# Attention weights of three batches: turned by VectorE in 32x32 blocks and moved through device memory, in place of TensorE transposes

## The chip, the core and the metric

The kernel runs on one core of a Trainium2 chip. Its time is the device time of one execution in microseconds; before the change three runs took 450.7, 450.86 and 450.96 us, with a median of 450.86 us. One execution was also recorded by the hardware profiler. The engines are TensorE (PE, with PEld for its weight loads), VectorE (DVE), ScalarE (ACT), GpSimd (POOL) and SyncE (SP), which here issues every DMA.

## The reference

The reference is block-sparse attention followed by a gated two-layer network. The shapes are 4 batches, 8 heads, 768 tokens, head size 64, model size 512 and inner size 1024, in float32.

```python
k_sum = k.reshape(B, H, nb, block, D).max(axis=3)       # block = 32, nb = 24
v_sum = v.reshape(B, H, nb, block, D).mean(axis=3)
scores = concat([where(|i - j| < 16, q k^T / 8, -1e9), q k_sum^T / 8 + log(32)], -1)
a = exp(scores - max); a = a / (a.sum(-1) + 1e-9)
attn = a @ concat([v, v_sum], axis=2)                    # heads side by side -> x
xk = mu_k * x + (1 - mu_k) * x_prev;  xr = mu_r * x + (1 - mu_r) * x_prev
out = sigmoid(xr @ w_r) * (square(relu(xk @ w_k)) @ w_v)
```

A token's local keys lie within 15 positions, so 64 queries need 96 keys and 24 block summaries: 120 columns in all.

## The kernel before, in words

The attention is cut into 32 units, one for each batch, pair of heads and half of the sequence (384 tokens). The function `unit` (from line 443) makes one. It computes scores on PE (L458, 24 small matmuls) with the queries on the 128 partitions and the 120 keys along the row, three slots of 128 queries for each of the two heads. DVE adds the mask and finds the row's extreme (L469), ACT takes the exponential and its sum (L473), DVE inverts the sums (L479, L480) and POOL scales the rows (L485, six instructions). The weights lie in `y`, queries on the partitions. The product with the values needs keys on the partitions, so PE transposes the weights against an identity, two groups of three for a unit (L492, into the PSUM tile `pt`), and ACT copies each group to the tile `pts` (L496). PE then multiplies with the values (L505, 24 small matmuls), and DVE or ACT copies the result `av` into the tile `vx` that holds the tokens x (L516, L518).

The network works on halves of a batch: seven halves use the split form, in which each float32 operand is a sum of a high and a low part and three matmuls stand for one product. For a half there are a gate (L562 to L564, three groups of 12 matmuls), eight first products (L601, 12 matmuls each) and eight second products (L628, 9 each). ACT and DVE make the high and low parts of the activations (L542, L544, L614 to L616) and of the weights (L341, L344). The first half of batch 0 is partly plain: its gate (L575) and the products with an index below the two numbers `PLAIN` use the unsplit operands, 4 matmuls for a first product and 3 for a second. Plain float32 matmuls leave two records each in the profile, split ones one.

The kernel has no fixed order of its own. Every piece is declared to a planner (`Plan`, L106) with its engine, an estimated length, the tiles it reads and writes, and a due time; the planner plays the program through once and emits each engine's instructions in the order that it found. That order is then kept by the hardware: an engine whose next instruction must wait does nothing else. Constants at the top (L39 to L71) set the due times: `GATE0`, `GATE1` and `PERIOD` for the gates, `STEP0` and `STEP` for the products, `FIRST`, `SECOND` and `UNITS` for the units. The units of batch 1 to 3 are computed while the network works on the batch before. Matmuls on a tile of zeros (`warm`, L682) are put into gaps of PE that the planner foresees early on.

SP issues loads of k, v, q and vT (L359, L363, L441, L408), weights (L323) and stores of the output (L662). For batches 1 to 3 the block means of v are computed from the extra load vT and written into the windows of `vx` by two small DMAs for each set (L432, which spreads 24 rows over six windows).

## Time and profile before

| | |
|---|---|
| median of 3 runs | 450.86 us |
| profiled execution, its own time | 450.6 us |
| its span from first to last instruction | 448.8 us |
| PE busy | 441.7 us (98%) |
| ACT busy | 282.9 us (63%) |
| DVE busy | 261.2 us (58%) |
| POOL busy | 104.8 us (23%) |
| granted TensorE clock, mean | 1.000 |

The profiled time is 1.8 us longer than the span, for what lies around the first and the last instruction. PE's records overlap, because matmuls are pipelined, so the mean length of a matmul record (278 ns for a transpose) is longer than the distance from one start to the next. The distance between starts is what a matmul adds to a busy PE. In the rows of the timeline and of the chain of waits the first number is a start and the second a length, both in us.

### The profile page before, as it was taken

To read this page: it belongs to the slowest core of one execution; us is meant where nothing else is said; L and a number is where in the kernel's file an instruction comes from. 1 tells how busy PE (TensorE), PEld (TensorE's weight loads), DVE (VectorE), ACT (ScalarE), POOL (GpSimd) and SP (SyncE) were. 2 spreads that over 40 slices of the span, in tenths; PEclk is the share of its full clock that TensorE was granted. 3 is DMA by queue.
4 is the path that set the end of the run, shared out by engine and by line. 5 is a ranking of instruction groups with operands and counts; after the bars stand their busy time and mean duration, and the time that the engine had idled before them with its cause. 6 is when DMAs were issued, how large, how long until landed. Compare 5 with 4: busy or idle time off the path is not lost.

```text
span 448.8 us, 9629 instructions
## 1 busy us (share of the span) xinstructions
PE 441.7 (98%) x3521; PEld 366.3 (82%) x3521; DVE 261.2 (58%) x866; ACT 282.9 (63%) x808; POOL 104.8 (23%) x237
## 2 busy tenths in 40 slices
PE   8999999999999999999999999999999999999996
PEld 8755578778888888978888888987888888888895
DVE  3889998995645763194655756175663455232213
ACT  3798999997765583288866655268966555232221
POOL 0561545561540012032432012002442001000000
PEclk9999999999999999999999999999999999999999
DMA  8967886831024275051007076031000010001001
GB/s 288 395 225 253 318 300 225 273 136 39 15 71 150 77 246 200 2 169 31 15 2 272 2 243 229 0 125 64 15 15 15 1 71 1 1 0 72 0 0 72
DMA packets 24230, 51.96 MB, mean 116 GB/s; under 512 B 2935, under 2 KB 10743, under 8 KB 24183
## 3 DMA queue, kind: packets, MB, share of 16 engines
q1 hardware_dynamic: 24183, 51.35, 33.3%
q8 instruction: 28, 0.46, 0.4%
q14 instruction: 19, 0.16, 0.1%
HBM read 43.28 MB, written 6.29 MB: 110 GB/s over the span
## 4 chain that ended last, share of the span: by engine, by line
PE 90%; ACT 3%; DMA 3%; DVE 2%; SPq 1%; issue 0%; DVEq 0%
PE mm L628 30%; PE mm L601 29%; PE av L505 5%; PE pt L492 5%; PE sc L458 4%; PE mm L562 4%; PE mm L564 4%; PE mm L563 4%; DMA vx<-in_v 3%; PE mm L575 2%; ACT y L473 1%; PE pt L412 0%; DVE z L658 0%; ACT pts L496 0%; PE mm L397 0%
## 5 line engine op out<-in xcount | busy, mean ns | idle before, releaser
L601 PE MATMUL mm<-xs,w 128*128 128x384 f32 x756 | 147.4, 343 | 0.0
L601 PEld LDWEIGHTS mm<-xs,w 128*128 128x128 f32 x756 | 132.9, 188 | 7.4 <-issue 0.7
L485 POOL TENSOR_SCALAR y<-y,rc 128x120 f32<-128x120 f32 x192 | 83.9, 455 | 142.1 <-DVE rc L480 117.1
L628 PE MATMUL mm<-w,kh 128*128 128x512 f32 x366 | 100.3, 402 | 0.2 <-ACT kh L615 0.2
L608 ACT ACTIVATE r<-mm 128x384 f32<-128x384 f32 x64 | 31.3, 489 | 95.7 <-PE mm L601 95.7
L473 ACT ACTIVATE y<-y,mn 128x120 f32<-128x120 f32 x192 | 73.7, 387 | 13.2 <-DVE mn L469 13.1
L628 PEld LDWEIGHTS mm<-w,kh 128*128 128x128 f32 x366 | 66.1, 188 | 12.6 <-ACT kh L615 0.5
L614 DVE CAST kh<-r 128x384 fp32r<-128x384 f32 x55 | 21.1, 384 | 92.6 <-ACT r L610 83.6
L628 PE MATMUL mm<-w,kl 128*128 128x512 f32 x183 | 57.0, 406 | 0.0
L469 DVE CUSTOM_DVE_ANT_0 y<-sc,mask_sb 128x120 f32<-128x120 f32 x192 | 42.5, 276 | 16.1 <-PE sc L458 16.0
L544 DVE TENSOR_TENSOR xs<-xa,xs 128x384 fp32r<-128x384 f32 x56 | 30.5, 551 | 32.8 <-ACT xs L542 32.6
L628 PEld LDWEIGHTS mm<-w,kl 128*128 128x128 f32 x183 | 32.9, 188 | 7.4 <-issue 0.5
L533 DVE SCALAR_TENSOR_TENSOR xa<-vx,mu_sb,xa 128x384 f32<-128x384 f32 x56 | 33.5, 627 | 8.2 <-POOL xa L530 4.2
L616 DVE TENSOR_TENSOR kl<-r,kh 128x384 fp32r<-128x384 f32 x61 | 34.7, 569 | 4.2 <-ACT kh L615 0.7
L473 ACT ACTIVATION_READ_ACCUMULATOR y<-y,mn 128x1 f32 x192 | 36.4, 189 | 0.0
L610 ACT ACTIVATE r<-r 128x384 f32<-128x384 f32 x64 | 33.7, 526 | 1.2
L505 PEld LDWEIGHTS av<-pts,vx 120*64 120x64 f32 x768 | 25.1, 137 | 10.2 <-issue 6.4
L562 PE MATMUL mm<-w,xs 128*128 128x512 f32 x84 | 33.3, 397 | 0.0
L492 PE MATMUL pt<-ident_sb,y 128*120 128x128 f32 x192 | 32.5, 278 | 0.8 <-ACT pts L496 0.6
L496 ACT COPY pts<-pt 120x384 f32<-120x384 f32 x64 | 30.1, 470 | 5.0 <-PE pt L492 4.3
L564 PE MATMUL mm<-w,xs 128*128 128x512 f32 x84 | 32.9, 392 | 0.0
L563 PE MATMUL mm<-w,xs 128*128 128x512 f32 x84 | 32.8, 390 | 0.0
(65 smaller groups left out, 505.1 us busy)
## 6 DMA issues: line engine op xcount, KB each, us to landing
vx<-in_v SPq DMA_DIRECT2D x32, 384.0 KB
kt<-in_k SPq DMA_DIRECT2D x15, 544.0 KB
qt<-in_q SPq DMA_DIRECT2D x32, 192.0 KB
out<-z SPq DMA_DIRECT2D x24, 256.0 KB
st<-in_vT SPq DMA_DIRECT2D x12, 384.0 KB
st<-in_w_k SPq DMA_DIRECT2D x8, 512.0 KB
st<-in_w_v SPq DMA_DIRECT2D x8, 512.0 KB
st<-in_w_r SPq DMA_DIRECT2D x4, 512.0 KB
```

What stands on the lines that cost most here:

```text
L469: op("DVE", "mask", None, lambda h=h, i=i, var=var: nc.vector.tensor_tensor_reduce(out=y[h].t[:, i, :], in0=sc[h].t[:, i, 0:NK], in1=mask_ ...
L473: op("ACT", "exp", None, lambda h=h, i=i: nc.scalar.activation(y[h].t[:, i, :], y[h].t[:, i, :], AF.Exp, bias=mn[h].t[:, i:i + 1], scale=-1.0,
L485: op("POOL", "norm", None, lambda h=h, i=i: nc.gpsimd.tensor_scalar(out=y[h].t[:, i, :], in0=y[h].t[:, i, :], scalar1=rc.t[:, NSL * h + i: ...
L492: nc.tensor.transpose(out=pt[h].t[0:NK, i * P:(i + 1) * P], in_=y[h].t[:, i, :], identity=ident_sb)
L505: nc.tensor.matmul(av.t[hs, w * QW:(w + 1) * QW], windows(vw)[:, w, hs], pts[h].t[:, i, c * QW:(c + 1) * QW], start=True, stop=True,)
L562: nc.tensor.matmul(ps.t, xh.t[:, ts], h, start=(p == 0), stop=False)
L563: nc.tensor.matmul(ps.t, xh.t[:, ts], l, start=False, stop=False)
L564: nc.tensor.matmul(ps.t, xl.t[:, ts], h, start=False, stop=(p == NPAIR - 1))
L601: nc.tensor.matmul(ps.t[:, 0:HT], w.t[:, p * P:(p + 1) * P], x[p][s].t, start=(n == 0), stop=(n == len(terms) * NPAIR - 1))
L610: op("ACT", "square", None, lambda: nc.scalar.activation(r.t, r.t, AF.Square), reads=[(r, 0)], writes=[(r, 0)])
L616: op("DVE", "sub", None, lambda: nc.vector.tensor_tensor(out=kl.t, in0=r.t, in1=kh.t.bitcast(F32), op=ALU.subtract), reads=[(r, 0), (kh, 0 ...
L628: nc.tensor.matmul(acc[t].t, a.t[:, t * P:(t + 1) * P], v.bitcast(F32) if single else v, start=start, stop=stop)
```

## The change

For batches 1 to 3 the six PE transposes and the two ACT copies of a unit are gone. In their place stand:

- two DVE instructions (`flip`, new line 514), one for each head, each of which turns the 12 blocks of 32x32 in a 128x384 tile. The `y` tiles grow from 120 to 128 columns, so that they divide by 32, and POOL clears the eight added columns once. The turned blocks go into a tile of the pool `st`, which the loads of weights and of vT use too.
- four stores (`put`, new line 523), each from 32 partitions to a scratch tile in device memory (`far`, four tiles), 128 runs of 768 bytes each. The place in the scratch does what the block transpose leaves undone: it exchanges the blocks.
- one load (`get`, new line 527) of the 128 x 3072 bytes back into `pts`, which is now one tile for both heads, with two tiles in turn.

Batch 0 keeps the PE transposes. Its copies write the new arrangement of `pts`, and the products with the values read each 64 queries as two runs of 32.

The planner's numbers change too: `PLAIN` goes from 3 to 6, so that three more first and three more second products of the first half are plain; the steps, periods and gaps of the due times change; and the scores of batches 1 to 3 are due 22 us ahead of their unit's time, in place of 10.

```diff
-STEP0 = 4000
-PLAIN = 3, 3
-GATE1 = 76000
-PERIOD = 50000
-STEP = 4600
-SLACK = 400
+STEP0 = 5200
+PLAIN = 6, 6
+GATE1 = 84000
+PERIOD = 52000
+STEP = 4400
+SLACK = 800
...
-GAP = 300
+GAP = 500
...
+AHEAD = 22000
+ISSUES = dict(put=720, get=400, spread=820)
...
-UNITS = 5500
+UNITS = 8500
...
-        op("PE", "score", due - 10000, scores, reads=[*e["kparts"], (kt, "s"), (qt, 0)],
+        op("PE", "score", due - (10000 if b == 0 else AHEAD), scores, reads=[*e["kparts"], (kt, "s"), (qt, 0)],
...
+            if b > 0:
+                continue
             op("PE", "transpose", due - 3500 + 800 * h, transposes,
                reads=[(y[h], i) for i in range(NSL)] + [*IDENT], writes=[(pt[h], 0)])
             op("ACT", "pts", None, lambda h=h: nc.scalar.copy(
-                out=pts[h].t, in_=pt[h].t[0:NK, 0:NSL * P].rearrange("p (i c) -> p i c", c=P)),
-               reads=[(pt[h], 0)], writes=[(pts[h], 0)])
+                out=pts.t[0:NK, :, h].rearrange("p a i q -> p i a q"),
+                in_=pt[h].t[0:NK, 0:NSL * P].rearrange("p (i a q) -> p i a q", i=NSL, a=4)),
+               reads=[(pt[h], 0)], writes=[(pts, h)])
+        spots = [(pts, h) for h in range(2)]
+        if b > 0:
+            yt = buf("st", U32, False)
...
+            for h in range(2):
+                op("DVE", "flip", due - AHEAD + 8000 + 600 * h, lambda h=h: nc.vector.transpose(
+                    out=turned()[:, :, h], in_=y[h].t.rearrange("p i (r c) -> p r i c", r=4)),
+                   reads=[(y[h], i) for i in range(NSL)], writes=[(yt, h)])
+            far = buf("far")
...
+            for c in range(4):
+                op("SP", "put", due - 8000 - ISSUES["put"] * (3 - c), lambda c=c: nc.sync.dma_start(
+                    out=rows()[:, :, c], in_=turned()[32 * c:32 * c + 32].rearrange("p r h i q -> p r (h i q)")),
+                   reads=[(yt, 0), (yt, 1)], writes=[(far, c)], size=32 * 3072)
+            spots = [(pts, "all")]
+            op("SP", "get", due - 4500, lambda: nc.sync.dma_start(
+                out=pts.t.rearrange("p c h i q -> p (c h i q)"), in_=far.t.rearrange("p c n -> p (c n)")),
+               reads=[(far, c) for c in range(4)], writes=spots, size=P * 3072)
...
-                        av.t[hs, w * QW:(w + 1) * QW], windows(vw)[:, w, hs], pts[h].t[:, i, c * QW:(c + 1) * QW],
+                        av.t[hs, w * QW:(w + 1) * QW], windows(vw)[:, w, hs], pts.t[0:NK, 2 * c:2 * c + 2, h, i],
```

The order of the instructions moves with it. On PE, in the network's second half of batch 1 while a unit of batch 2 is computed, the order before has this stretch: one group of transposes, six matmuls of a second product, the other group, and the next unit's scores.

```order
L492 MATMUL pt_130<-ident_sb,y_93 120x128 x3
L628 MATMUL mm_133<-w_0_616,kh_119 128x512
L628 MATMUL mm_133<-w_0_688,kh_119 128x512
L628 MATMUL mm_135<-w_0_616,kh_119 128x512
L628 MATMUL mm_135<-w_0_688,kh_119 128x512
L628 MATMUL mm_132<-w_0_616,kh_119 128x512
L628 MATMUL mm_132<-w_0_688,kh_119 128x512
L492 MATMUL pt_130<-ident_sb,y_94 120x128 x3
L458 MATMUL sc_128<-kt_61,qt_65 64x120 x2
```

In the changed program the same kind of stretch holds the products with the values (new line 536) alone among the network's matmuls.

```order
L659 MATMUL mm_130<-w_0_720,kh_117 128x512
L659 MATMUL mm_130<-w_0_751,kh_117 128x512
L659 MATMUL mm_132<-w_0_720,kh_117 128x512
L659 MATMUL mm_132<-w_0_751,kh_117 128x512
L659 MATMUL mm_133<-w_0_720,kh_117 128x512
L659 MATMUL mm_133<-w_0_751,kh_117 128x512
L536 MATMUL av_129<-pts_105,vx_70 64x64 x12
L659 MATMUL mm_130<-w_0_720,kl_119 128x512
```

The 48 transpose groups of batches 1 to 3 are gone from PE; what the values wait for is now a load.

On SP the units' DMAs stand among the others. This is the piece in which the first two units of batch 2 are put out and loaded back (`far` and `pts` are the scratch and its destination; `vx<-vm` spreads the block means).

```order
L523 DMA far_136<-st_121 32x4x192 x4
L527 DMA pts_104<-far_136 128x768
L523 DMA far_137<-st_122 32x4x192
L436 DMA vx_76<-vm_87 24x6x128
L523 DMA far_137<-st_122 32x4x192 x3
L436 DMA vx_79<-vm_87 24x6x128
L412 DMA st_121<-in_vT 128x768
L445 DMA qt_66<-in_q 128x384
L527 DMA pts_105<-far_137 128x768
```

SP issues 286 DMAs in place of 166: 96 stores and 24 loads are added and none of the others is taken away. SP too keeps its order: a load back waits for its four stores, and whatever stands behind it on SP waits with it.

On DVE the turns stand between the network's work. This piece is from the same two units (`kl` is the low part of an activation that a second product needs, `sm` and `rc` the sums of the second unit).

```order
L514 STREAM_TRANSPOSE st_121<-y_93 128x4x96
L647 TENSOR_TENSOR kl_119<-r_115,kh_117 128x384
L514 STREAM_TRANSPOSE st_121<-y_91 128x4x96
L483 TENSOR_SCALAR sm_100<-sm_100 128x6
L484 RECIPROCAL rc_103<-sm_100 128x6
L645 CAST kh_116<-r_114 128x384
L647 TENSOR_TENSOR kl_118<-r_114,kh_116 128x384
L514 STREAM_TRANSPOSE st_122<-y_92 128x4x96
```

A turn waits for POOL's scaling of its tile, and the low parts behind it in the queue wait with it. Counted over the whole order, DVE gets 48 turns; copies of `av` on DVE go from 12 to 4 and on ACT from 20 to 28, casts of activations on DVE from 55 to 41 and on ACT from 6 to 17; ACT's copies to `pts` go from 64 to 16.

More of the change, by code (lines that the diff above doesn't have):

```diff
@@ L184, in schedule @@
                         continue
-                    start, need, ok = max(at, now, o.due - EARLY if e == "SP" else 0), {}, True
+                    start, need, ok = max(at, now, o.due - EARLY if e == "SP" and o.name not in ("put", "get") else 0), {}, True
                     if e == "SP":
@@ L228, in schedule @@
             if e == "SP":
[L229 removed]
+                engines[e] = start + ISSUES.get(o.name, ISSUE)
                 dma = max(dma, start + 600) + o.size * DMA_NS_PER_BYTE
@@ L446, in unit @@
         sm, rc = buf("sm"), buf("rc")
-        pt = [buf("pt") for _ in range(2)]
-        pts = [buf("pts") for _ in range(2)]
+        pts = buf("pts")
+        pt = [buf("pt") for _ in range(2)] if b == 0 else None
         av = buf("av")
```

29 lines of the change are left out of this document (18 added, 11 removed).

## The prediction

> **What bounds the kernel now.** I read the page's head and its chain of waits first, then busy time by stretches, then the waits of PE.
>
> ```profile
> span 448.8 us, 9629 instructions
> PE 441.7 (98%) x3521; PEld 366.3 (82%) x3521; DVE 261.2 (58%) x866; ACT 282.9 (63%) x808; POOL 104.8 (23%) x237
> PE 90%; ACT 3%; DMA 3%; DVE 2%; SPq 1%; issue 0%; DVEq 0%
> ```
> ```profile
> 0.00:40.00 40.00, 37.72 (x443) 27.02 (x444) 30.30 (x105) 27.85 (x88) 14.47 (x36) 1.00 0.81 291
> 40.00:100.00 60.00, 59.13 (x520) 42.77 (x519) 58.11 (x203) 57.43 (x178) 31.20 (x56) 1.00 0.74 257
> 100.00:350.00 250.00, 250.00 (x2083) 213.24 (x2083) 139.49 (x494) 164.50 (x479) 57.81 (x146) 1.00 0.27 90
> 350.00:446.00 96.00, 94.81 (x480) 83.26 (x478) 33.26 (x66) 33.09 (x66) 1.32 (x1) 1.00 0.06 20
> ```
> ```profile
> PE mm L628 <- ACT kh L615: 0.2, 1, 0.2
> ```
>
> The columns of the stretches are the stretch, then busy time of PE, PEld, DVE, ACT and POOL, the clock, the DMA share and GB/s. From 100 us on PE has no gap, and the last row, PE's only wait between 100 and 446 us, is 0.2 us. So there a microsecond of PE work taken away is a microsecond gained, as long as nothing makes PE wait instead. From 40 to 100 us PE, DVE (58.11 of 60) and ACT (57.43) are all full. Before 40 us loads rule (DMA share 0.81) and PE is padded with warm matmuls. The clock is 1.00 in all four.
>
> **What goes: 48 transpose groups on PE.** One transpose group is three matmuls; its price is a distance of starts, not the 278 ns of a record.
>
> ```profile
> 106.45 0.49 PE L492 MATMUL pt<-ident_sb,y 128*120 128x128 f32 x3
> 106.87 0.85 PE L458 MATMUL sc<-kt,qt 64*64 64x120 f32 x24
> 329.27 0.85 PE L458 MATMUL sc<-kt,qt 64*64 64x120 f32 x24
> 330.04 0.92 PE L505 MATMUL av<-pts,vx 120*64 120x64 f32 x24
> 330.89 0.96 PE L628 MATMUL mm<-w,kl 128*128 128x512 f32 x3
> 331.69 0.49 PE L492 MATMUL pt<-ident_sb,y 128*120 128x128 f32 x3
> 331.94 2.33 PE L601 MATMUL mm<-xs,w 128*128 128x384 f32 x12
> 334.11 0.49 PE L492 MATMUL pt<-ident_sb,y 128*120 128x128 f32 x3
> ```
>
> The group costs 0.25 us (331.69 to 331.94) to 0.42 us (106.45 to 106.87). It also makes its neighbours a little longer: the first product behind it takes 2.17 us (331.94 to 334.11) where 2.11 is usual. A second reading bounds the whole from above, by the period of a batch with units and the stretch without any:
>
> ```profile
> 253.97 0.39 PE L562 MATMUL mm<-w,xs 128*128 128x512 f32 x1
> 358.68 0.39 PE L562 MATMUL mm<-w,xs 128*128 128x512 f32 x1
> 444.64 0.40 PE L628 MATMUL mm<-w,kl 128*128 128x512 f32 x1
> ```
>
> One batch takes 104.7 us (253.97 to 358.68). The last batch, which has no units beside it, takes 86.4 us (358.68 to 445.0), of which about 2.1 us is a second product left from the batch before: 84.3 us. Eight units with their four means thus cost 20.4 us. Scores are 0.77 (329.27 to 330.04) and values 0.85 (330.04 to 330.89), 13.0 us for eight; with some 0.8 us for the means 6.6 us are left for 16 groups, 0.41 us each. I take 0.36, between the 0.32 that the middle of 0.25 and 0.42 gives and 0.41: 48 x 0.36 = **17.3 us** off (15.4 to 19.7).
>
> **What comes on PE: PLAIN from 3 to 6.**
>
> ```profile
> 41.73 2.58 PE mm L601 x8
> 47.86 2.58 PE mm L628 x6
> 169.12 2.10 PE mm L628 x9
> 171.21 2.11 PE mm L601 x12
> ```
>
> These pieces of the chain are a plain first and second product (2.58 us each) and split ones (2.11 and 2.10). Three of each: 3 x (0.47 + 0.48) = **2.85 us** on. Against it three fewer high and low parts are made on the crowded DVE; I count nothing for that, since the new order puts the turns of batch 1 and earlier scores into the same time.
>
> **What comes on DVE, and what leaves ACT.** The trace shows no block transpose. Its nearest rows are elementwise instructions of the same 128x384:
>
> ```profile
> L616 DVE TENSOR_TENSOR kl<-r,kh 128x384 fp32r<-128x384 f32 x61 | 34.7, 569 | 4.2 <-ACT kh L615 0.7
> L614 DVE CAST kh<-r 128x384 fp32r<-128x384 f32 x55 | 21.1, 384 | 92.6 <-ACT r L610 83.6
> L516 DVE COPY vx<-av 128x384 f32<-128x384 f32 x12 | 6.7, 555 | 8.1 <-PE av L505 8.1
> L496 ACT COPY pts<-pt 120x384 f32<-120x384 f32 x64 | 30.1, 470 | 5.0 <-PE pt L492 4.3
> ```
>
> Between 384 and 569 ns I take 0.56 us, the slow end, because blocks are no plain stream: 48 x 0.56 = 27 us on DVE. The planner moves 8 copies (8 x 0.555) and 14 casts (14 x 0.384) off DVE, 9.8 us. DVE then has about 278 us of work in some 437, and ACT, without 48 copies of 0.47 (22.6 us), has less than before. Neither bounds the whole; PE's 100 to 350 us cover this work, where DVE was busy 139 of 250. If the cover failed it would be by a turn that waits for POOL while the low parts queue behind it, and then PE waits for those. In the piece of the order shown the turns come after the next unit's masks, so POOL has had that time.
>
> [...]
>
> **The new way from scores to values.** Here a wait can take the place of the work. The old chain of one unit, and the nearest DMAs:
>
> ```profile
> 337.65 0.85 PE L458 MATMUL sc<-kt,qt 64*64 64x120 f32 x24
> 341.88 2.46 POOL L485 TENSOR_SCALAR y<-y,rc 128x120 f32<-128x120 f32 x6 [5.48 <-DVE rc L480]
> ```
> ```profile
> L432 SPq DMA_DIRECT2D vx<-vm x24: 778/786/949, 83.3 to 339.9; - x24
> 0.74 0.86 SPq L359 DMA_DIRECT2D kt<-in_k  x2
> 3.36 0.55 DVE L373 TENSOR_REDUCE kg<-kt 128x24 f32<-128x384 f32 x1 [3.36 <-DMA kt<-in_k]
> 4.20 0.55 DVE L373 TENSOR_REDUCE kg<-kt 128x24 f32<-128x384 f32 x1 [0.21 <-DMA kt<-in_k]
> 445.09 1.03 SPq L662 DMA_DIRECT2D out<-z  x2
> ```
>
> Scores start at 337.65 and POOL ends at 344.34: 6.7 us. The second turn adds 0.56 and perhaps 0.3 in DVE's queue: 7.6. Four stores follow. The nearest issue is the spread of the means, 786 ns for 24 x 6 runs (a put has 128 runs), so the last store is issued 2.4 us after the first. How long a DMA takes: a load of 280 KB, issued at 0.74, woke DVE at 3.36, 2.6 us; with the second part, 544 KB, it was 4.20, 3.5 us; the last stores of 256 KB, issued by 446.1, were over by the span's end at 448.8, at most 2.7 us. A store of 96 KB lies below the loads by its size, and with its longer issue I take 2.5 us (2.1 to 2.7). The load back of 384 KB lies between the two loads; I take 2.9 us (2.6 to 3.5). Sum: 7.6 + 2.4 + 2.5 + 2.9 = 15.4 us, about 15.7 with semaphores.
>
> SP can add to it: one or two spreads of 0.79 stand between a unit's stores and its load, so 16.5 to 17.3 us; and where a sigmoid came before, ACT loads its table for exponentials first (1.28 us):
>
> ```profile
> L473 ACT ACT_TABLE_LOAD x9 | 11.5, 1283 | 0.9 <-PEq L795 0.7
> ```
>
> Against that stands the PE work which the new order puts between the start of a unit's scores and its values. For the first unit of batch 2 it is three groups of scores (3 x 0.77), four first products (4 x 2.11), three and two thirds of second ones (3.67 x 2.10) and one means transpose (0.2): 18.7 us. Counted like this over all 24 units it is 17.5 to 23.7 us, 21 in the middle; the shortest is the fourth unit of batch 1. So the loads should land 1 to 4 us before they are needed, with little to spare in a few units. When PE waits once, the scores that are already out gain the same time, so a late load is not paid again by the units in flight. I put **1.5 us** for all such waits (0 to 8).
>
> **The start.** The order of the first 40 us is almost the same, with 44 warm matmuls for 39 and the same gate. The planner thus sees about five more small gaps there. Each warm matmul is two records:
>
> ```profile
> L682 PE MATMUL pt<-zero_sb 128*128 128x128 f32 x78 | 13.2, 323 | 1.6 <-POOL vx L514 1.0 <-ACT pts L496 0.6
> ```
>
> 13.2 us for 39 are 0.34 us each; five make 1.7 us at most, if none of it fills time that was idle anyway, and nothing if all of it does. I take **0.5 us**.
>
> **Sum.** The profiled execution took 450.6 us (span 448.8 and 1.8 around it). 450.6 - 17.3 + 2.85 + 1.5 + 0.5 = 438.15 us. The median of the three runs is 0.26 us above the profiled one, so I forecast **438.4 us**, 2.8% less.
>
> **Rivals.**
>
> *The load is late in many units.* If store and load take 1.5 us longer each than I put, the way is 19 to 20 us, and about half of the 24 units (those with under 21 us of PE work) are late by 1 us or a little less, some 8 to 10 us in place of 1.5: 446 us. For it: no row shows a load that follows a store to device memory, and SP's order puts other transfers ahead. Against: the DMA share is 0.27 from 100 to 350 us, so the queues are mostly empty.
>
> *SP becomes the bound, and the kernel is slower.* SP keeps its order, so the wait of each load back for its four stores holds the loads of q, k and v behind it; these feed the next scores, and the delay goes round. It decides from the point where the way exceeds the mean 21 us of PE work by over half a microsecond in every unit, that is when store and load together take about 11 us and not 5.4: 24 x 0.6 = 14 us eat the gain. At 1 us for each unit the sum is 438.4 - 1.5 + 24 = 461 us. Against it is the 2.7 us bound on a store above. [...]
>
> *The neighbours' time goes too, and nothing waits.* 48 x 0.41 off, no late loads, no loss at the start: 450.86 - 19.7 + 2.85 = 434.0 us.
>
> *The change does not do what it says* (the transposes stay on PE) is excluded by the new order: 48 PE transposes are left of 192, all of batch 0.
>
> **How the numbers follow.** The forecast (435.5 to 442 us) gets 0.58, late loads in many units 0.18, the better case 0.12, SP as the bound 0.12. A measurement of this kernel tells a change of about 0.2%, 0.9 us. Only the slower rival crosses that line, and its lower edge meets no change: faster 0.86, within it 0.04, slower 0.10. The range leaves out what lies above late loads and a little below the better case: 433.5 to 447.
>
> **What would show it.** PE's busy time should fall by about 14 us, the L601 and L628 rows should stay at their lengths, and PE's waits for the DMA of `pts` should sum to under 3 us. Turns should read 0.4 to 0.6 us and a put's issue about 0.75 us. The forecast is wrong if `values` wait for `pts` by more than a microsecond in most units, if DVE shows waits for POOL's `y` in front of `kl`, or if the first product starts more than 2 us later than 41.7 us.

## The result, and the profile after

The changed kernel takes 445.62 us (median of four runs, 444.78 to 447.34), against 450.84 us for the kernel before beside it: a ratio of 0.9889, 95% interval 0.9855 to 0.9923. It is faster by 5.2 us; the forecast was 12.4. The sign and the place of the gain were right, its size was more than twice too large. The profiled execution took 446.4 us, where the sum had been 438.15, so 8.25 us are to be found.

The head of the page and its chain of waits:

```profile
span 444.6 us, 9448 instructions
PE 433.3 (97%) x3366; PEld 351.4 (79%) x3366; DVE 274.5 (62%) x890; ACT 269.1 (61%) x772; POOL 109.4 (25%) x245
PE 80%; DMA 9%; ACT 6%; DVE 3%; issue 1%; SPq 0%; ACTq 0%
```

PE still sets the end, but its share of the chain fell from 90% to 80%, and DMA has 9% of it where it had 3%. None of these 9% are stores or loads back; the long pieces behind the start are loads of weights and of k and a spread (start, length):

```profile
54.10 5.84 DMA st<-in_w_k
64.06 4.88 DMA st<-in_w_k
82.08 5.13 DMA kt<-in_k
99.87 2.37 DMA vx<-vm
102.24 2.34 issue
```

From 47 to 99.8 us the chain has 18.8 us of ACT, the 15.9 us of these three loads, 8.0 us of PE and 7.8 of DVE; in the kernel before it has 37.3 us of PE there and no load. PE's busy time fell by 8.4 us (441.7 to 433.3), not by the 14 forecast. Busy time by stretches (stretch, then PE, PEld, DVE, ACT, POOL, the clock, the DMA share, GB/s):

```profile
40.00:100.00 60.00, 57.97 (x455) 35.89 (x455) 56.70 (x200) 54.80 (x173) 27.25 (x57) 1.00 0.78 252
100.00:350.00 250.00, 247.33 (x2010) 208.83 (x2010) 158.09 (x519) 156.15 (x451) 59.52 (x144) 0.99 0.54 165
100.00:110.00 10.00, 7.33 (x66) 5.64 (x66) 6.99 (x25) 7.53 (x25) 3.16 (x9) 0.83 0.70 193
```

From 100 to 350 us PE was busy for all 250 before; now 2.7 us are missing, all of them in the ten microseconds from 100 to 110, and there the granted clock is 0.83. The waits of PE say on what:

```profile
PE av L536 <- issue: 2.7, 1, 2.7
PE mm L606 <- DVE xs L564: 1.4, 1, 1.4
```

Of 24 products with the values that wait for a load back, one waited: the second unit of batch 1, for 2.7 us. Rows of PE's timeline around it (start, length; rows in between are left out):

```profile
104.57 1.02 PE L536 MATMUL av<-pts,vx 120*64 120x64 f32 x24 [2.67 <-issue]
105.53 1.22 PE L659 MATMUL mm<-w,kh 128*128 128x512 f32 x2
106.55 0.63 PE L659 MATMUL mm<-w,kl 128*128 128x512 f32 x1
106.97 0.63 PE L593 MATMUL mm<-w,xs 128*128 128x512 f32 x1
108.67 0.40 PE L594 MATMUL mm<-w,xs 128*128 128x512 f32 x1
110.52 0.62 PE L659 MATMUL mm<-w,kh 128*128 128x512 f32 x2
```

The matmuls behind the wait are slower than the same ones later (records of 0.63 against 0.40; 1.22 for two against 0.62). The seven from 105.53 to 108.67 take 3.14 us; at the later rate (0.23 from start to start) they take 1.60. So the wait cost 2.67 us and 1.5 more in a slow clock. Microsecond by microsecond the clock reads 0.62 from 105, 0.50 from 106 and from 107, 0.67 from 108 and 1.00 from 109.

The way of this unit from scores to values shows where it was late; its scores and its second turn are these rows:

```profile
80.80 0.85 PE L462 MATMUL sc<-kt,qt 64*64 64x120 f32 x24
91.66 0.57 DVE L514 STREAM_TRANSPOSE st<-y 128x384 f32<-128x384 f32 x1
```

From the start of the scores to the end of the second turn it takes 11.4 us (80.80 to 92.23), where the sum had 7.6. The whole way to the values takes 23.8 us (to 104.57), and without the wait there were 21.1 us of PE's time for it, the middle that the prediction had counted.

The new row of DVE among the groups of instructions, and from PE's timeline the two starts that bound a batch and PE's last matmul:

```profile
L514 DVE STREAM_TRANSPOSE st<-y 128x384 f32<-128x384 f32 x48 | 27.4, 572 | 11.0 <-POOL y L489 7.9 <-POOL vx L545 1.6 <-DMA qt<-in_q 1.2
```
```profile
254.28 0.39 PE L593 MATMUL mm<-w,xs 128*128 128x512 f32 x1
354.35 0.39 PE L593 MATMUL mm<-w,xs 128*128 128x512 f32 x1
440.49 0.40 PE L659 MATMUL mm<-w,kl 128*128 128x512 f32 x1
```

A turn takes 0.572 us and 48 take 27.4. A batch with units takes 100.07 us (254.28 to 354.35), where it took 104.71: 4.64 us for 16 groups, 0.29 each and not 0.36.

Last, the start, on PE and on DVE:

```profile
41.72 2.84 PE L606 MATMUL mm<-w,xs 128*128 128x512 f32 x6 [1.41 <-DVE xs L564]
44.40 2.74 PE L632 MATMUL mm<-xs,w 128*128 128x384 f32 x8
```
```profile
39.88 0.95 DVE L377 TENSOR_REDUCE kg<-kt 128x48 f32<-128x768 f32 x1 [1.04 <-DMA kt<-in_k]
41.80 2.20 DVE L564 SCALAR_TENSOR_TENSOR xs<-vx,mu_sb,xs 128x384 f32<-128x384 f32 x4
```

The first plain product starts at 44.40; before it was 41.56. DVE stood 1.04 us in front of a reduction over keys whose load had not landed, and the mixes (L564) that PE's gate needs were queued behind it. Not all of the 2.84 us is lost: ahead of this point PE now makes one unit's scores more (144 small matmuls in place of 120, 0.77 us), which it is spared later.

The two executions can be compared at three points: the first plain product, the first gate of batch 1 (the expectations below call it the first product of the second channel mix), and PE's end.

| kernel | first plain product | gate of batch 1 | from there to PE's end |
|---|---|---|---|
| before | 41.56 | 149.29 | 295.75 |
| after | 44.40 | 154.19 | 286.70 |

Behind the gate of batch 1 both kernels have the same matmuls, except for the 32 groups. There the change is a clean gain of 9.05 us, 0.28 for each group. Up to that gate it has lost 4.9 us, although 16 of the 48 groups lie there.

### The profile page after: what moved, and what is told of

The parts are those of the page before. It is cut to its first block, busy times and chain, and to the rows that moved or that the text cites. A ratio compares the mean times of both kernels' runs of the same rounds, so it can differ in the third digit from the quotient of the medians.

```text
span 444.6 us, 9448 instructions
## 1 busy us (share of the span) xinstructions
PE 433.3 (97%) x3366; PEld 351.4 (79%) x3366; DVE 274.5 (62%) x890; ACT 269.1 (61%) x772; POOL 109.4 (25%) x245
## 4 chain that ended last, share of the span: by engine, by line
PE 80%; DMA 9%; ACT 6%; DVE 3%; issue 1%; SPq 0%; ACTq 0%
PE mm L659 28%; PE mm L632 27%; PE av L536 5%; PE mm L593 4%; PE mm L595 4%; PE mm L594 4%; PE sc L462 4%; DMA st<-in_w_k 2%; ACT y L477 2%; DMA kt<-in_k 2%; PE mm L606 2%; DMA mu_sb<-in_mu 1%; DMA vx<-in_v 1%; DMA qt<-in_q 1%; ACT wc L328 1%
## 5 line engine op out<-in xcount | busy, mean ns | idle before, releaser
L632 PE MATMUL mm<-xs,w 128*128 128x384 f32 x744 | 149.1, 349 | 0.0
L632 PEld LDWEIGHTS mm<-xs,w 128*128 128x128 f32 x744 | 130.8, 188 | 10.5 <-issue 1.9
L489 POOL TENSOR_SCALAR y<-y,rc 128x120 f32<-128x120 f32 x192 | 85.4, 462 | 139.8 <-DVE rc L484 109.7
L659 PE MATMUL mm<-w,kh 128*128 128x512 f32 x348 | 94.6, 400 | 0.4 <-ACT kh L646 0.4
L659 PEld LDWEIGHTS mm<-w,kh 128*128 128x128 f32 x348 | 64.3, 189 | 13.1 <-ACT kh L646 0.7
L645 DVE CAST kh<-r 128x384 fp32r<-128x384 f32 x41 | 15.4, 375 | 69.8 <-ACT r L641 69.7
L659 PE MATMUL mm<-w,kl 128*128 128x512 f32 x174 | 54.4, 406 | 0.0
L561 POOL TENSOR_SCALAR xa<-vx,om_sb 128x384 f32<-128x384 f32 x16 | 12.4, 785 | 105.3 <-DVE xs L575 102.2
L647 DVE TENSOR_TENSOR kl<-r,kh 128x384 fp32r<-128x384 f32 x58 | 32.7, 564 | 7.2 <-ACT kh L646 4.4
L564 DVE SCALAR_TENSOR_TENSOR xa<-vx,mu_sb,xa 128x384 f32<-128x384 f32 x56 | 33.3, 619 | 2.7 <-ACT xa L558 2.7
L514 DVE STREAM_TRANSPOSE st<-y 128x384 f32<-128x384 f32 x48 | 27.4, 572 | 11.0 <-POOL y L489 7.9
```

What stands on the lines that cost most here:

```text
L489: op("POOL", "norm", None, lambda h=h, i=i: nc.gpsimd.tensor_scalar(out=y[h].t[:, i, 0:NK], in0=y[h].t[:, i, 0:NK], scalar1=rc.t[:, NSL * ...
L564: op("DVE", "mixd", None, lambda: nc.vector.scalar_tensor_tensor(out=xa.t, in0=xt.t[:, 1 + lo:1 + lo + HT], scalar=mu_sb[:, which, p:p + 1 ...
L632: nc.tensor.matmul(ps.t[:, 0:HT], w.t[:, p * P:(p + 1) * P], x[p][s].t, start=(n == 0), stop=(n == len(terms) * NPAIR - 1))
L647: op("DVE", "sub", None, lambda: nc.vector.tensor_tensor(out=kl.t, in0=r.t, in1=kh.t.bitcast(F32), op=ALU.subtract), reads=[(r, 0), (kh, 0 ...
L659: nc.tensor.matmul(acc[t].t, a.t[:, t * P:(t + 1) * P], v.bitcast(F32) if single else v, start=start, stop=stop)
```

## The experiments

In the diffs, `nth(name, n)` is the operation number n of that name in the planner's order (counted from 0) and `shift(o, at)` puts `o` right in front of `at`; the lines stand behind the call of the planner. For all new kernels the table gives these points in their profiles, the last as the distance from the gate of batch 1 to PE's end. "PE's waits" are those between 95 and 135 us, in order, in us. The ratio is to the kernel before, run beside each; that kernel's median moved between 449.83 and 450.84 us, so kernels of different rows are best compared by their ratios (0.9889 for the changed kernel). The points come from one execution of each kernel. e3, e5, e6, e9, e10 and e12 keep the changed kernel's order in the start, and yet their first plain product lies anywhere from 43.57 to 47.98; e3, with the same wait of PE, has its gate 1.7 us earlier than the changed kernel. Smaller differences of one point can't be read as an effect.

| kernel | median us | ratio, 95% interval | first plain product | gate of batch 1 | to PE's end | PE's waits |
|---|---|---|---|---|---|---|
| e1_no_transposes | 437.64 | 0.9733 (0.971 to 0.9755) | 40.93 | 143.88 | 286.70 | 0.48 |
| e2_double_transposes | 465.12 | 1.0329 (1.0311 to 1.0347) | 40.95 | 153.01 | 306.2 | |
| e3_load_first | 445.17 | 0.989 (0.9871 to 0.9909) | 43.91 | 152.49 | 286.71 | 2.73 |
| e4_means_late | 445.22 | 0.9888 (0.9869 to 0.9907) | 43.5 | 154.54 | 286.73 | 2.98 |
| e5_loads_behind | 449.67 | 0.9976 (0.9959 to 0.9992) | 44.91 | 156.18 | 286.7 | 4.37 |
| e6_warm_in_gap | 444.49 | 0.9865 (0.984 to 0.989) | 44.16 | 152.88 | 286.71 | 0.33, 0.17, 1.03 |
| e7_plain3 | 448.37 | 0.9954 (0.993 to 0.9977) | 45.94 | 158.09 | 286.7 | 0.36, 0.36, 0.34, 1.78 |
| e8_new_numbers_alone | 455.2 | 1.0101 (1.0079 to 1.0123) | 42.84 | 156.3 | 293.4 | |
| e9_no_late_wait | 444.32 | 0.9877 (0.9857 to 0.9898) | 43.57 | 152.91 | 286.7 | 0.40, 1.25, 1.30, 0.92 |
| e10_v_load_behind | 445.19 | 0.99 (0.9879 to 0.9921) | 44.32 | 152.76 | 286.71 | 0.15, 0.37, 1.47, 0.69 |
| e11_path_alone | 445.69 | 0.9909 (0.989 to 0.9929) | 41.08 | 152.27 | 287.89 | 0.50 |
| e12_stores_first | 444.9 | 0.9864 (0.9838 to 0.989) | 47.98 | 154.68 | 286.68 | 0.25, 0.96, 0.91 |
| e13_start_and_stores | 444.89 | 0.9875 (0.985 to 0.99) | 44.22 | 154.34 | 286.70 | 0.52, 1.78 |
| e14_no_wait_in_four | 445.3 | 0.9886 (0.9859 to 0.9912) | 43.44 | 151.77 | 286.69 | 0.98, 1.72 |

**What a group is worth.** First the old kernel without the transposes of batches 1 to 3, then with each of them made twice.

```diff
-                for i in range(NSL):
+                for i in range(NSL if b == 0 else 0):                # e1
+                for i in list(range(NSL)) * (1 if b == 0 else 2):    # e2
                     nc.tensor.transpose(out=pt[h].t[0:NK, i * P:(i + 1) * P], in_=y[h].t[:, i, :], identity=ident_sb)
```

> The kernel before, with the PE transposes of batches 1 to 3 left out and nothing in their place (ACT still copies the old content of the PSUM tile, so the attention of these batches is not computed rightly). It prices the 48 groups alone. Theory A (a group is worth 0.29 us on a busy PE, as the period of a batch in the two profiles says: 104.7 against 100.1 us, 4.6 for 16 groups): 450.8 - 13.8 = 437.0 us, 436 to 438. Rival B (a group is worth the 0.36 us of the prediction, and the change loses the rest because PE's other work became slower beside the added DMAs or with the two-run operand): 450.8 - 17.3 = 433.5 us, and the period of a batch near 99 us.

> The kernel before, with each group of transposes of batches 1 to 3 issued twice in a row: 48 groups more on PE, the same result. Theory A: the second three of a group cost their bare distance of starts, about 0.25 us or less, since the switch to a transpose and back is paid already: 450.8 + 12 = 463 us or a little less. Rival B (0.36 us each): 468 us. If the cost is 0.29 and there is no switch cost: 465 us.

Without them the time falls by 12.6 us, with them doubled it rises by 14.9 (465.12 against 450.26): 0.26 to 0.31 us for a group. The period of a batch says the same:

```profile
244.01 0.39 PE L562 MATMUL mm<-w,xs 128*128 128x512 f32 x1
344.19 0.39 PE L562 MATMUL mm<-w,xs 128*128 128x512 f32 x1
```
```profile
262.93 0.39 PE L562 MATMUL mm<-w,xs 128*128 128x512 f32 x1
372.85 0.39 PE L562 MATMUL mm<-w,xs 128*128 128x512 f32 x1
```

100.18 us without, 104.71 in the kernel before, 109.92 with twice as many: (104.71 - 100.18) / 16 = 0.28 and (109.92 - 104.71) / 16 = 0.33. The price rises a little with the number, so a group that is removed is worth the lower end. From the gate of batch 1 to the end, e1 and the changed kernel have the same matmuls and take the same 286.70 us to the hundredth. So in two thirds of the program the new way costs PE nothing at all, and everything else that is missing is lost before that gate. That excludes the rivals that spoke of many late loads and of SP as the bound.

e1 shows one thing more. Its gate of batch 1 stands 5.4 us earlier than in the kernel before (143.88 against 149.29), 4.8 us earlier counted from the first plain product, for the 16 groups of batch 1. This execution is the fastest of its five, 1.5 us below their median, but of the median's 12.6 us, too, some 3.6 are left beside the 9.05 behind the gate. So ahead of the gate PE work that is taken away is time gained as well; what is lost there comes with what stands in its place.

**The late load.** The second unit's stores were issued from 92.94 to 95.1 us, and its load back only at 100.84, behind a spread of block means. This experiment put the load back ahead of that spread.

```diff
     order = plan.schedule()
+    get = nth("get", 1)
+    shift(get, [o for o in order[:order.index(get)] if o.name == "spread"][-1])
```

> The changed kernel with one SP instruction moved: the load back of the second unit of batch 1 is issued ahead of the spread of the block means that stood in front of it and waited. Theory A (the 2.7 us wait of PE at 101.8 us comes from the order on SP, and the slow clock of the 4 us behind it comes from that wait): 445.6 - 2.7 - 1.6 = 441.3 us, 440.8 to 442.5, no PE wait over 1 us near 102 us and a clock of 1.00. Rival C (the load lands late because the stores and the queues are slow, not because of its place): 444.5 to 446, with the wait still over 1.5 us.

The wait stayed at 2.7 us. SP's queue in this run (start, length, line, operation):

```profile
90.21 0.43 SPq L367 DMA_DIRECT2D vx<-in_v  x1
90.68 0.43 SPq L412 DMA_DIRECT2D st<-in_vT  x1
91.16 2.34 SPq L523 DMA_DIRECT2D far<-st  x4
93.59 1.65 SPq L436 DMA_DIRECT2D vx<-vm  x2
97.25 0.36 SPq L445 DMA_DIRECT2D qt<-in_q  x1
99.64 0.34 SPq L527 DMA_DIRECT2D pts<-far  x1
```
```profile
102.86 1.15 PE L536 MATMUL av<-pts,vx 120*64 120x64 f32 x24 [2.73 <-DMA pts<-far]
```

The load back left as soon as the stores were through, and that was at 99.64, 6.1 us after the last of them was issued. I had put 2.5. In front of the four stores stand two loads of 393 KB each. The load itself then took 3.2 us (99.64 to 102.86; I had put 2.9).

To see whether these two loads hold up the stores, they were put behind the load back, which also stands ahead of the spread as in e3:

```diff
+    lo, hi = order.index(nth("get", 0)), order.index(nth("get", 1))
+    at = order[hi + 1]
+    for o in [o for o in order[lo:hi] if o.name == "load" and o.size >= P * 768 * 4]:   # e10: of these the load of v
+        shift(o, at)
```

> The changed kernel with three SP instructions moved: the loads of v and vT (0.75 MB) that stood ahead of the four stores of the second unit of batch 1 are issued behind its load back, and that load stands ahead of the spread, as in the run e3_load_first. In that run the load back still waited 1.7 us for the stores and PE 2.7 us for the load. Theory E (the stores take 6 us because they queue behind loads in the DMA engines): PE's wait near 100 us falls under 0.7 us, the clock stays at 1.00, and the time is 445.2 - 2.7 - 1.6 = 440.9 us, 440 to 442.5. Rival F (the turns or the trip itself are late whatever stands ahead): wait over 1.5 us, 444 to 446 us.

> The changed kernel, with the 393 KB load of v (tile vx_78) alone moved on SP from in front of the four stores of the second unit of batch 1 to behind that unit's load back, and that load back put ahead of the spread of the means in front of it. The equally large load of vT stays where it was, ahead of the stores, so the block sums on VectorE that wait for it are not late as they were when both loads were moved. Theory A: the stores come back after half of the queued bytes, about 4 us after their issue and not 6; the load back lands some 2 to 3 us earlier, the values wait 0.5 us at most, the 2.7 us and the slow stretch behind it are gone: 441.5 to 442.5 us, ratio near 0.98. Rival B: the trip of the stores is set by the vT load and the others in flight just the same: the wait stays above 1.5 us and the time at 444.5 to 445.5. Rival C: the v load is now late itself for the channel mix that needs it, and a wait of 2 us or more shows on a row of L564 or L575 and then on PE: 446 or more.

SP's queue in e5 and in e10:

```profile
92.33 1.80 SPq L523 DMA_DIRECT2D far<-st  x4
97.57 0.34 SPq L527 DMA_DIRECT2D pts<-far  x1
```
```profile
92.40 2.40 SPq L523 DMA_DIRECT2D far<-st  x4
98.75 0.34 SPq L527 DMA_DIRECT2D pts<-far  x1
```

From the end of the stores' issue to the load back it is 6.1 us with 786 KB of loads ahead (e3), 4.0 with 393 KB (e10), 3.4 with neither (e5); for the last unit of the changed kernel, when hardly anything else moves, it is 1.6 from its last store (336.60 to 338.21; the other three had left 3 us earlier). So the loads that SP issued before the stores hold them up, and the two loads are worth 2.7 of the 6.1 us. That is a part of the cause that I had left out; what makes the 3.4 of the rest, against 1.6, was not traced.

But mending it brought nothing. In e5 the kernel is 4 us slower than the changed one, with a new wait:

```profile
PE mm L659 <- DVE kl L647: 4.4, 1, 4.4
```
```profile
105.17 0.95 DVE L413 TENSOR_REDUCE vs<-st 128x24 f32<-128x768 f32 x1 [5.19 <-DMA st<-in_vT]
107.26 0.52 DVE L647 TENSOR_TENSOR kl<-r,kh 128x384 fp32r<-128x384 f32 x1
```

The load of vT was now late, DVE stood 5.19 us in front of its block sums, and the low part that PE needed was queued behind them. In e10, where vT stays in front, the wait of the second unit's values is 0.15 us and the clock is 1.00, and yet the time is 445.19: the third, fourth and fifth unit wait now, 0.37, 1.47 and 0.69 us, with the 0.15 again 2.7 together.

**Without the wait.** The values of the second unit read the tile of the unit before it, so that PE can't wait for that load; the product with this unit's own weights is left out. Later four units were freed in this way.

```diff
         own, mine.place = mine.place, other.place   # e9, values number 9: "other" is the tile of the unit before
         values_only()                               # e14, values 9 to 12: a view of zero_sb, and the edit of e4
         mine.place = own
```

> The changed kernel, in which the values of the second unit of batch 1 alone read the weights tile of the unit before it, which landed long ago (so that unit's output is wrong, and nothing else is left out). The stores and the load of that unit stay where they are; only PE's wait for them is gone. Theory A: the one late load cost 2.7 us of waiting and, by the records of about half speed behind it, some 1.6 us more, so 4.3 us of what is missing came from it: 445.6 - 4.3 = about 441.3 us, ratio near 0.979, the clock near 1.00, and the first product of the second channel mix starts near 150 us and no longer at 154.2. Rival B: VectorE and ScalarE are full until 100 us and set the pace there, so PE arrives at the next low or high part too early and waits for it instead: 444 us or more, with a new wait of 2 us or more on a row of L606, L659 or L462 between 103 and 112 us.

> The changed kernel with the block means late, and with the values of the second to fifth unit of batch 1 multiplied by a tile of zeros that is there from the start in place of the weights from device memory (so the outputs of these four units are wrong; the scores, turns, stores and loads of them all remain). PE then waits for no store or load before 122 us. Account 1 (the way): all 4.3 us of wait and slow clock go, and nothing comes back behind them: the first product of the second channel mix starts 149.5 to 150.5 us, 441.5 to 442.5 us in all, ratio near 0.981. Rival (VectorE and ScalarE set the pace): PE then waits 2 us or more for the low or high parts or for scores' masks between 98 and 125 us, and the time stays above 443.5 us.

I expected e9 to give back 4.3 us. By the ratios it gave 0.5 (0.9877 against 0.9889, with overlapping intervals), by the medians, taken beside kernels before that differ by 1.0 us, 1.3. The wait came back behind it:

```profile
110.44 0.92 PE L536 MATMUL av<-pts,vx 120*64 120x64 f32 x24 [1.25 <-ACT xs L573]
114.32 0.92 PE L536 MATMUL av<-pts,vx 120*64 120x64 f32 x24 [1.30 <-issue]
120.53 0.92 PE L536 MATMUL av<-pts,vx 120*64 120x64 f32 x24 [0.92 <-DMA out<-z]
```

With four units freed (e14) PE runs without a gap to 125 us, and then waits 0.98 us for the sixth unit's values and 1.72 for a high part from DVE: 2.7 us once more. The busy times of the stretch before, in e14:

```profile
40.00:60.00 20.00, 19.72 (x119) 11.01 (x112) 19.33 (x65) 19.29 (x57) 7.10 (x17) 1.00 0.87 307
60.00:80.00 20.00, 20.00 (x129) 10.80 (x127) 18.60 (x57) 19.14 (x52) 6.38 (x12) 1.00 0.75 247
80.00:100.00 20.00, 20.00 (x238) 15.56 (x239) 19.38 (x81) 18.32 (x74) 13.56 (x30) 1.00 0.71 210
```

From 40 to 100 us PE, DVE and ACT are each busy for more than nine tenths of the time, and the DMA engines for 0.71 to 0.87. What PE is spared at one place it meets at the next in these runs; that full DVE and ACT are the reason is not shown. In e1 they are as full (58.02 and 58.41 of 60 us), and yet the gate of batch 0's second half stands at 92.37 where it was at 94.85. Both times lie on the side of the rivals (444.3 and 445.3 us), but the waits are mostly not where the rivals put them: in e9 most stand on the values, in e14 behind 125 us.

**Warm matmuls in the gap.** Ten matmuls on zeros in front of the late values keep PE busy while it waits.

```diff
+        for _ in range(10):
+            nc.tensor.matmul(spare, zero_sb, zero_sb, start=True, stop=True)
         values()                                    # of the second unit of batch 1
```

> The changed kernel with ten more warm matmuls on PE (zeros, 2 to 2.5 us) just ahead of the late product with the values, so that PE isn't idle while it waits. Theory G (the slow clock of the 4 us behind the wait comes from PE's idleness): the records behind run at full pace, clock 1.00, and the time falls by about 1.6 us to 443.8 us, 443 to 444.5. Rival H (the clock falls for another reason, or the warm matmuls add as much as they save): 445 to 446.5 us.

The clock of the stretch is 1.00 and the time 444.49, 1.1 us less than the changed kernel, which is of the size of the 1.5 us read off the slow matmuls; the intervals overlap. Over the whole execution the clock was 0.999 or 1.000 in all six runs of e6. The changed kernel had 1.000 in one of four, at 444.84 us, and 0.996 in its fastest, at 444.78, so the price of the slow clock is read off the trace and not shown in the times. Here is the stretch that had 7.33 and 0.83:

```profile
100.00:110.00 10.00, 9.67 (x93) 8.25 (x90) 7.75 (x28) 7.54 (x20) 3.03 (x8) 1.00 0.71 187
```

**The start.** The block means of the late keys are put behind the five mixes on DVE.

```diff
+    kred = nth("kred", 3)
+    fifth = [o for o in order if o.name == "mixd" and order.index(o) > order.index(kred)][4]
+    at = order[order.index(fifth) + 1]
+    for o in chain:                        # kred and the three operations that use what it makes
+        shift(o, at)
```

> The changed kernel with one chain of DVE instructions moved: the block maxima of the first set of batch 1 (which wait for a load of k that lands at 39.9 us) are issued behind the five mixes of tokens that the last gate group and the first products need. Theory A (2.3 us of the late start come from DVE's queue): PE's wait of 1.4 us at 40.3 us goes and the first plain product starts near 42.8 us in place of 44.4; 445.6 - 1.5 = 444.1 us. Rival D (between 40 and 100 us DVE and ACT set the pace, so a start gained is lost again before 100 us): 445 to 446 us, the first gate of the second half at 98 us as before.

PE's wait in front of the gate is gone and the first plain product stands at 43.5, 0.9 us earlier; but e9, with the changed kernel's order on DVE, has it at 43.57. The next gate, of batch 0's second half, stood at 98.13 us, as in the changed kernel (98.07). What was won at the start was lost again before 98 us.

**The planner's numbers.** Three kernels: the changed one with three plain products in place of six, the old one with all the new numbers, and the changed one with all the old numbers except the lead of the scores.

```diff
-PLAIN = 6, 6
+PLAIN = 3, 3                      # e7: the changed kernel, this line only
```

> The changed kernel with PLAIN back at 3, all else as changed; the planner lays out the order anew. Theory A (a plain product costs PE 0.47 to 0.48 us more, and PE sets the pace): 2.85 us less, 442.4 us, 441.5 to 443.5. Rival D (from 40 to 100 us DVE and ACT set the pace, and the plain form spares them three casts and subtractions and puts off splits of weights): no gain or a loss, 445 to 448 us, with more waits of PE before 100 us.

> The kernel before, transposes on PE, with the planner's new numbers (PLAIN 6, steps, period, gap, slack, units) and without the new path. If the numbers cost only the plain products: 450.3 + 2.85 = 453.1 us, 452.5 to 454. If they also bring the late start and the later first 100 us (theory A's 2.3 to 3 us): 455 to 456.5 us with a first product near 44 us. If they spread the work better than the old ones: 449 to 451 us.

> The changed kernel with the numbers of the kernel before for the start, the gates, the slack and the units (4000, 3 and 3, 76000, 50000, 4600, 400, 300, 5500); the block transposes, the stores and the load back stay, and with them the lead of 22000 of a unit's scores. Theory A: the numbers cost 4.6 us in the old kernel and as much here, so without them 445.6 - 4.6 = 441 us, and values still wait in one unit only. Rival B: three plain products only, with batch 1 begun as early as before: the load of VectorE and ScalarE from 40 to 100 us pushes the low parts late, as in the run with three plain products (448.4), and several values wait for their load, because the units lie closer together: 447 to 455 us, with PE waiting for DMA or issue of the values' row in five units or more.

Three plain products fewer should save 2.85 us of PE work; e7 is 2.8 us slower. Between 80 and 120 us PE makes 29 matmuls on zeros there (two records each), 7.5 us, that the planner put where it foresaw nothing to do; the changed kernel has 3, 0.8 us. Besides, PE waits 1.78 us for values in front of 106.11 us. So the work that PE was spared went into filler and a wait, and a plain product, which needs no high and low part, pays for itself here. The planner laid out the whole order of e7 anew, so that the reason, full DVE and ACT, is argued and not shown.

In the old kernel the new numbers cost 4.6 us (e8), so the way itself is worth some 9.6 (455.2 to 445.62). In the changed kernel the old numbers neither cost nor save clear of noise (445.69; 0.9909 against 0.9889). Its start is 3.3 us earlier, as before the change, so the numbers have a part in the late start (e8, with the numbers alone, starts 1.3 us later than before); but PE then has 27 matmuls on zeros between 80 and 120 us (54 records), 7.1 us:

```profile
80.00:100.00 20.00, 5.06 (x38) 4.70 (x39) 1.00 0.77 221
100.00:120.00 20.00, 2.03 (x16) 1.65 (x15) 1.00 0.70 202
```

By the planner's reckoning these are waits, though the page counts them as busy. e1, with the same numbers and no new way, has no such matmul in this stretch, and neither has the kernel before. So e11 against e1 prices the new way ahead of the gate: from the first plain product to the gate of batch 1 it takes 111.19 us in place of 102.95, some 8 us more, of which the filler is 7.1. My expectation of 441 us added two effects that seem to take the place of one another.

**Both ends at once.** In e9 and e10 the third unit's weights were turned by 96.5 and 97.6 us, and its stores left at 101.1 and 100.6, behind the second unit's load back on SP, which waited for its own stores. In e12 the stores of the fourth and fifth unit stand ahead of the load back of the unit before, and those of the third right behind the second's; e13 adds the late means of e4.

SP's order there is now this (on top of e10's edit):

```
L527 DMA pts_105<-far_137 128x768
L523 DMA far_138<-st_122 32x4x192 x4
L436 DMA vx_75<-vm_85 24x6x128
L367 DMA vx_78<-in_v 128x768
L523 DMA far_139<-st_120 32x4x192 x4
L527 DMA pts_104<-far_138 128x768
L436 DMA vx_78<-vm_85 24x6x128
L523 DMA far_136<-st_121 32x4x192 x4
L527 DMA pts_105<-far_139 128x768
L527 DMA pts_104<-far_136 128x768
L693 DMA out<-z_106 128x512
```

> The kernel of the run with the v load behind, with SP's order from the load back of the second unit of batch 1 to that of the fifth written anew: the four stores of the third unit right behind the load back of the second, those of the fourth ahead of the load back of the third, those of the fifth ahead of the load back of the fourth, and the load back of the fifth ahead of the output stores and v loads; the spreads and the v load stand in between as before. Nothing is left out, and the other engines keep their order. Theory A (SP's order): in the two runs before, the weights of the third unit were turned at 96.5 us and its stores went out only at 100.6 to 101.0, behind a load back that waited for its own stores; from unit to unit each load back held the next unit's stores, and PE waited 0.4 to 1.5 us at three to four units between 101 and 121 us. With the stores ahead the third unit's leave at about 99 and the fourth's at 102.5, the loads land 1 to 3 us before they are needed, these waits sum to under 0.8 us, the first product of the second channel mix starts at 150.5 to 151, and the time is 442.5 to 443.2 us, ratio near 0.983. Rival B (the trips): the stores take 4 to 6 us and the loads 3 to 4 because the DMA engines are at 0.7 to 0.99 there; then sending them earlier only lengthens the queue, the waits stay above 1.8 us together, and the time stays at 444.5 to 445.5 us.

> The kernel of the run with the stores first, and with the block means of the key load put behind the five channel mixes on VectorE, as in the run with the means late. Nothing is left out. Account 1 and 2 together: the first plain product starts at 43.5 us instead of 47.98, the stretch from it to the first product of the second channel mix stays at the 106.7 us of the run with the stores first, so that one starts near 150.2, and the rest of the program is 286.7 us long as in every kernel: the profiled run takes 442.4 us, ratio near 0.982. Rival: what is won at the start is lost again before 98 us, as with the means late alone, because VectorE and ScalarE are full from 40 to 100 us: 444 to 445 us, ratio 0.986 to 0.988.

In e12 the values wait 0.25 and 0.96 us, and from the first plain product to the gate of batch 1 it takes 106.70 us, 3.1 less than in the changed kernel. But the median is 444.9. The profiled execution is the slowest of its six (446.86; the others 443.52 to 444.93), and it is late at the other end:

```profile
43.60 3.93 PE L606 MATMUL mm<-w,xs 128*128 128x512 f32 x5 [2.47 <-DVE xs L564]
```
```profile
41.77 0.95 DVE L377 TENSOR_REDUCE kg<-kt 128x48 f32<-128x768 f32 x1 [2.10 <-DMA kt<-in_k]
```

The load of the keys took 6.1 us from its issue in this execution (35.70 to 41.77) and 5.0 in the changed kernel's (34.88 to 39.88), and the first plain product slid to 47.98. The other engines had that time as well, so the 3.1 us can't be put down to the order of the stores. With the start mended too (e13), PE meets no late values until 125.97 us, and then waits 1.78 us for a high part, with the clock at 0.93 from 125 to 150:

```profile
131.67 2.25 PE L659 MATMUL mm<-w,kh 128*128 128x512 f32 x6 [1.78 <-DVE kh L645]
```

The gate of batch 1 stands at 154.34 again, 110.12 us behind the first plain product: the 3.1 us are gone. Both times fell on the side of the rivals, though the waits of the values in e12 add up to 1.2 us and not to the rival's 1.8. No variant is shown to beat the changed kernel: by the ratios e6 and e12 lie 1.1 us below it and e9 and e13 0.5 to 0.6, within the intervals.

## Why the prediction was right or wrong

**PE sets the end, and a microsecond taken from it is a microsecond gained: right for what was taken away, but the condition "as long as nothing makes PE wait instead" failed before 150 us.** From the gate of batch 1 on, the changed kernel equals the kernel without transposes. Ahead of it e1 gained its 16 groups too, so the rule itself held there. In the kernel before, 12 of these 16 groups stand between 104.03 and 138.81 us; from 100 to 125 us DVE was busy for 15.07 of 25 us and the DMA engines for 0.11, and the changed kernel has 18.26 and 0.72 there. With the old numbers the new way costs some 8 us ahead of the gate, 7.1 of them as filler (e11 against e1). I had quoted the row of the full stretch, 40 to 100 us (58.11 and 57.43 of 60), and drawn nothing from it for the new way, which begins in it.

**The transpose groups, 48 x 0.36 = 17.3 us: mis-sized.** Measured are 0.28 to 0.29 each for removal, 13.7 us (12.6 by the medians of e1): 3.6 us of the miss. The starts in the trace (0.25 to 0.42) were a good reading, and their middle of 0.32 is near the doubled run's 0.33. What pulled it up was the second reading, 0.41 from the difference between a batch with units and a stretch without. It put everything left over to the transposes; the runs show that some 0.12 us for each group belongs to something else in the units. A remainder bounds a price only from above.

**PLAIN, 2.85 us: right as PE work, wrong as a term.** A plain product takes 2.58 us in the changed kernel as well. But e7, without three of each, is 2.8 us slower, not faster, with 7.5 us of filler. I had counted the relief of DVE at nothing; that this relief is what e7 lacks is argued.

**Turns, copies and casts: right.** 0.572 us against 0.56, 27.4 us against 27; DVE ends at 274.5 busy (278 forecast). DVE does wait for POOL in front of turns (7.9 us in 12 places), which I had named as a sign of failure, but no low part that PE needed was late by it.

**Waits for the load back, 1.5 us: the count was right, the size wrong.** One unit in 24 waited, which is fewer than I feared, but with the clock it cost 4.2 us, not 1.5. Three steps failed. The way from scores to turned weights was taken from a quiet moment, 7.6 us, and is 11.4 in the late unit. So was the way of a store (2.5 us; 1.6 when quiet in this trace as well), and it is 4.0 us with 393 KB of loads ahead (e10) and 6.1 with 786 KB (e3); the stretch before 100 us had shown a DMA share of 0.74 in the prediction's own table. And behind the wait of 2.67 us seven matmuls took 3.14 us in place of 1.60, which nothing in the profile before could show, since PE's longest wait there is 1.0 us. The 0.3 us that the sum of the way had for semaphores is shown by no run; a store that waited for a turn was issued 0.03 us behind the turn's end (changed kernel, 330.56 + 1.26 to 331.85).

**The start, 0.5 us: wrong.** The first plain product is 2.8 us later (44.40 against 41.56), of which 0.8 is a unit's scores made earlier and 2.1 is lost. I had called the order of the first 40 us almost the same, counted warm matmuls only and not looked at what stands in front of the mixes on DVE: that wait is 1.4 us. With it gone (e4) the start is still at 43.5, so the rest stays open. The prediction had named this as a sign that it was wrong: a first product over 2 us later.

Together, in the profiled execution: 3.6 for the groups, 1.6 for the start beyond 0.5, 2.7 for the late load and its clock beyond 1.5, 7.9 us, against 8.25 that were missing. This nearly adds up, but e4 and e9 to e14 show that the last two are no independent prices. Each can be taken away, and by the ratios 1.1 us at most come back, within the noise. Of the rivals, late loads in many units (446 us) has nearly the right time by the wrong mechanism.

What stays open: which engine holds PE back between 40 and 130 us. DVE, ACT and SP's order each show as the last wait in one run or another. The chain of the changed kernel names more: two loads of w_k (5.84 and 4.88 us) and the load of k at 82.08 (5.13 us), with ACT and DVE between them. This goes with the planner's new numbers: from 47 to 99.8 us e8 has 12.7 us of weight and key loads in its chain, e11, with the old numbers, 42.0 us of PE (filler included). No experiment moved these loads. A kernel with less DVE and ACT work in that stretch would tell too, and wasn't tried. Nor was another part of the change, three tiles for the block means (`vm`) in place of four.

## What to carry to other kernels

Price what goes and what comes in its place apart, each in its own stretch: here the removal alone gained in every stretch (e1), and the new way lost that again in the stretch in which it began, as waits or as filler, and filler reads as busy (7.1 us in e11). A way through device memory is priced with the transfers that the same queue was given before it, not with a DMA of a quiet moment (here 6.1 us against 1.6), and a load back that waits for its stores also holds whatever stands behind it on that queue (in e9 the third unit's stores, turned by 96.5 us, left at 101.1). When one wait is removed and the time does not move, look for the same microseconds on the next rows before looking for another cause.

## What the runs showed of the hardware

Behind some short waits of PE its clock was lower. After waits of 2.67 us (changed kernel), 2.73 (e3) and 2.47 (e12, at the start) the clock of the stretch of 10 us read 0.83, after 4.37 (e5) 0.90, and after 1.78 (e13) 0.93 over 25 us. The matmuls behind were up to twice as long (1.22 us for two against 0.62 in the changed kernel), and as long after a wait of 2.98 (e4). After 2.16 (e7, at the start, read over 40 to 100 us), 1.78 (e7), 1.72 (e14), 1.47 (e10) and 1.30 (e9) the clock read 1.00. A wait of 1.78 us was found on both sides, so its length alone doesn't decide; what else does, no run shows. With the ten matmuls on zeros of e6 in the gap the clock read 1.00 where the changed kernel had 0.83.

The last piece (98 KB) of a store took 1.6 us to be through in a quiet stretch (changed kernel, 336.60 to 338.21), and four pieces 6.1 us behind 786 KB of loads of the same queue (e3, 93.50 to 99.64). Each piece was issued in 0.43 us (median), where 0.79 had been taken from the spread of the means.
